# Holding back up to four score maxima to stand between dependent small VectorE instructions

## The chip, the cores and the metric

The kernel runs on one core of a Trainium2 chip. The metric is the device time of one execution in microseconds; the time of a kernel is the median of its runs. Lower is better.

## The reference

The program is attention that keeps the 32 largest scores of each row, followed by a mixture of experts with one expert per token. Shapes: q, k, v are 8 batches x 8 heads x 576 tokens x 64; eight experts of 512 x 1024 and 1024 x 512; all in float32.

```python
scores = scale * np.matmul(q, k.transpose(0, 1, 3, 2))
kth = np.partition(scores, -top_k, axis=-1)[..., -top_k:-top_k + 1]
mask = scores >= kth
scores = np.where(mask, scores, -1000000000.0)
...
attn = np.exp(scores)
attn = attn / (np.sum(attn, axis=-1, keepdims=True) + 1e-09)
return np.matmul(attn, v).astype(np.float32)
...
logits = x @ w_gate + modality_bias[modality_id]
e_idx = np.argmax(logits, axis=1)
...
    h = np.maximum(x[mask] @ w1[e], 0.0)
    out[mask] = gate_w[mask, None] * (h @ w2[e])
```

## The kernel before

The 64 heads are worked on as 32 pairs of heads of nine tiles each: 288 tiles of 128 query rows by 576 scores. One main loop takes one step per tile (line 846); the engines work on different tiles in the same step, by fixed offsets. In step i TensorE multiplies the scores of tile i+2 (`qk`, L324) and transposes the probabilities of tile i-9 (`trans`, L414); ScalarE makes the signs K of tile i-3 (`sign`, L369), the exponentials of tile i-6 (`expo`, L393) and copies the scores of tile i+2 to SBUF (`sevac`, L330); VectorE works on the score tile i. The attention output of a pair follows (`av`, L443), and whole experts of the mixture are fed to TensorE in the loop as soon as enough tokens are routed; a budget per step decides how many of their matrix products are issued (lines 931 to 942), by a table of costs and not by what runs late. After the loop (from about 1100 us) come the last batch's routing and the remaining expert slots.

The 32nd largest score of each row is found in parts. A row of 576 scores is cut in seven parts, and VectorE takes the eight largest of each (`subs`, L337, seven `MAX8` of 82 or 83 elements into `cand`, 56 candidates). In the next step the `chain` of that tile runs over the candidates: a `MAX8`, a replacement of the values found, a `MAX8`, a replacement, a `MAX8` (L348 to L350), each reading what the one before wrote. On the chip a replacement is two instructions, a load of the eight values (`MATCH_VALUE_LOAD`) and the replacement. GpSimd scales the 24th value (`below`, L362), ScalarE counts and signs with it, GpSimd multiplies scores and signs to `y` (L375), and VectorE takes the last eight maxima of `y` (`find`, L379). Every third step `pick` (L386 to L388) selects the threshold of three tiles with three small instructions, `eq`, `jk`, `kth`, each reading what the one before wrote. Last in every step `keep` (L399) compares the 576 scores with the threshold `kth` and multiplies with the exponentials; it writes the probabilities P.

The order on VectorE is written out by the loop (lines 949 to 982). `a_` holds the five instructions of the chain, `b_` the seven maxima, with `find` in its third place and the copies that came late (`lo`), and `c_` the step's end: `pick`, small instructions of the routing and of the choice of the next expert (`small_`, put at every second place, some of them DMAs or work of other engines), and `keep`. `weave` (L806) puts `a_` and `b_` into each other, one chain instruction first and then its share of `b_`; then `c_` runs as it stands:

```python
weave(a_, b_)
for f in c_:
    f()
```

The tile framework keeps this order on each engine and adds semaphore waits where an instruction reads what another one writes, on the same engine too. Score tiles lie in ten buffers (L329), the score PSUM tile in one, K in two, `y` in three. So ScalarE's copy of tile i+2 waits until VectorE's `keep` of tile i-8 has read the buffer's old tile.

Of the kernel before, what the change touches and what calls it, by code (L numbers as in the profile page):

```python
# [32 lines left out]
PJ = (0, 1, 3)  # L33
VJ = 7
QL = 2
KW = 8
KL = 2
LY = KL + 2
# [31 lines left out]
def kernel(  # L70
# [171 lines left out]
    def routing_loads():  # L242
        for h in range(2):
            SP.dma_start(wgt[h * 64:h * 64 + 64, :, h * E:h * E + E],
                         wg.rearrange("(a h p) e -> h p a e", h=2, p=64)[h])
        SP.dma_start(mbt, bass.AP(tensor=mb.tensor, offset=mb.offset, ap=[[0, 128], [E, 2], [1, E]]))
        pad_rows(E)
        return load_mod(0, B)
# [62 lines left out]
    def qk(i, p, j, bd):  # L311
        d = PR[p]
        ps = psS.tile([128, 2, 512], FT, name="S")
        for hf in range(2):
            a, b = hf * 288, hf * 288 + 288
            if j < 8:
                c, h = divmod(j, 2)
                terms = [(d["qs"][:, h, c * 128:(c + 1) * 128], x, h, a, b, 0) for x in range(2)]
            else:
                terms = [(bd[0], x, 0, a, b, 0) for x in range(2)]  # L320
                for u, v, o in ((a, min(b, 512), 64), (512, b, -512)):
                    terms += [(bd[1], x, 1, u, v, o) for x in range(2)] if u < v else []
            for n, (l, x, h, u, v, o) in enumerate(terms):
                PE.matmul(ps[:, hf, u - a:v - a], l, d["ks"][:, x, h, u + o:v + o], start=(n == 0),  # L324
                          stop=(n == len(terms) - 1), skip_group_check=(j == 8))
        T[i] = {"ps": ps}

    def sevac(i):
        T[i]["S"] = sb = wk.tile([128, S], FT, name="Ssb", bufs=LR + 1 + QL - QO)  # L329
        A.activation(sb.rearrange("p (a b) -> p a b", a=2), T[i]["ps"][:, :, :288], AF.Copy, scale=0.125)  # L330
# [64 lines left out]
    def keep(i, dn):  # L395

        t = T[i]
        probs(i)
        V.scalar_tensor_tensor(t["P"], t["S"], kth[:, i:i + 1], t["ex"], op0=OP.is_ge, op1=OP.mult, accum_out=dn)  # L399
# [5 lines left out]
    def probs(i):  # L405

        c, h = divmod(i % 9, 2)
        T[i]["P"] = Pm[:, :S] if c == 4 else Pb[c % 2][:, h * S:h * S + S]
# [15 lines left out]
    def av(p, j, x):  # L424

        vm, vt = LD[p]["v"]
        w = 256 if j < 8 else 64
        st = {}

        def part(c0, c1):  # L430
            if c0 == 0:
                st["po"] = psX.tile([128, 256], FT, name="X")
            po = st["po"]
            for c in range(c0, c1):
                for h in range(2):
                    K = slice(0, 128) if c < 4 else slice(64, 128) if h and j < 8 else slice(0, 64)
                    l = vm[:, h, c, :] if c < 4 else vt[K, h, :]
                    if j < 8:
                        r = PT[K, j // 2 - 1:j // 2 + 1, c + 5 * h if c < 4 else 4, :]
                    else:  # L440
                        r = PT[K, 1, 4 + c, h * 64:h * 64 + 64]
                    o = po[h * 64:h * 64 + 64, :w]
                    PE.matmul(o.rearrange("p (a b) -> p a b", a=2) if j < 8 else o, l, r, start=(c == 0), stop=(c == 4))  # L443
            if c1 == 5:
                o = (j // 4) * 256
                xev.append(lambda: A.activation(x[:, o:o + w], po[:, :w], AF.Copy))
        cut = {3: AV3, 7: AV7, 8: (0, 5)}[j]
        return [((b - a) * COST["av" if j < 8 else "av8"], lambda a=a, b=b: part(a, b)) for a, b in zip(cut, cut[1:])]
# [357 lines left out]
    def weave(a, b):  # L806

        nb, na, kb = len(b), len(a), 0
        for x in range(na):
            a[x]()  # L810
            e = (x + 1) * nb // na
            while kb < e:
                b[kb]()
                kb += 1
        while kb < nb:
            b[kb]()
            kb += 1

    def keep_warm(n):

        ps = psE.tile([128, 512], FT, name="E")
        for _ in range(2 * n):
            PE.matmul(ps[:, :256], onesb, idf.bitcast(BF), start=True, stop=True)
# [11 lines left out]
    modality = routing_loads()  # L835
    keep_warm(KW)
    for x in range(QL):
        qk(x, 0, x, qbd[0])
        sevac(x)
    ok = lambda x: 0 <= x < NT  # L840
# [5 lines left out]
    for i in range(LAST):  # L846
# [8 lines left out]
        def scores():  # L855
            if ok(i + QL):
                pp, jj = divmod(i + QL, 9)
                qk(i + QL, pp, jj, qbd[pp % 2])

        if ok(i + QL):  # L860
            cost += COST["mix" if (i + QL) % 9 == 8 else "qk"]
# [58 lines left out]
        if avs:  # L920
            c, f = avs.popleft()
            f()
            cost += c
        if ok(u) and u % 9 in (3, 7, 8):
            f = av(u // 9, u % 9, xTs(u // 36)[(u // 9) % HP])
# [6 lines left out]
        while seen[0] and spare_pe > 0:  # L932
# [4 lines left out]
            c, f, new = moe[0]  # L937
# [11 lines left out]
        a_, b_, c_ = [], [], []  # L949
# [11 lines left out]
        for x in range(RN if rush else 0):  # L961
            f = rush.popleft() if rush else PAUSE
# [6 lines left out]
        for x in range(SN - len(small_)):  # L969
            f = side.popleft() if side and not rush else PAUSE  # L970
# [6 lines left out]
        if ok(i - LR):  # L977
            u = i - LR
            c_.append(lambda u=u: keep(u, den[(u // 36) % 2][:, (u // 9) % HP, u % 9:u % 9 + 1]))
        weave(a_, b_)  # L980
        for f in c_:
            f()
# [269 lines left out]
```

## Time and profile before

| | |
|---|---|
| runs | 1340.63, 1344.9, 1348.74 us |
| median | 1344.9 us |
| the profiled execution | 1345.19 us, of which the span from first to last instruction is 1343.4 us |
| TensorE matmul busy | 1227.5 us (91%) |
| VectorE busy | 1174.4 us (87%) |
| ScalarE busy | 1001.1 us (75%) |
| GpSimd busy | 630.0 us (47%) |
| mean granted TensorE clock | 0.976 of full |

The profile is one execution, recorded by the hardware profiler. An instruction has a start and a duration; on VectorE the next one can start while the one before is still finishing, so the distance between two starts can be shorter than the duration, and the sum of durations is not the time that the engine needs. The views used below are the busy time by stretch, the lists of waits (who waited for whom, by semaphores) and the timeline, which gives each instruction's start and duration. In the rows PE is TensorE (PEld its weight loads), DVE VectorE, ACT ScalarE, POOL GpSimd and L a line of the kernel; [0.73 <-DVE P L399] behind an instruction says how long its engine had been idle and what ended that; in a list of waits the three numbers are the sum in us, how many, and the longest.

### The profile page before, as it was taken

The numbers are of one execution on the slowest core, as the hardware profiler recorded it, in microseconds if no ns is written. First come the engines' busy times: TensorE is split into PE (matmuls) and PEld (weight loads), VectorE is DVE, ScalarE is ACT, GpSimd is POOL, SyncE is SP. The second block draws the span as 40 slices with busy tenths as digits, with TensorE's granted clock in tenths as the row PEclk, the third lists the DMA queues.
The fourth block names the chain that finished last, engine by engine and source line by source line (L and its number), as shares of the span: only waits on it lengthen the run. The fifth ranks groups of instructions, "written<-read, shape, count | busy, mean of one in ns | idle before, by whom it ended". The sixth has DMA issues, their size and how long they took to land. (4 is left out here: it accounts for less than half of the span.)

```text
span 1343.4 us, 28995 instructions
## 1 busy us (share of the span) xinstructions
PE 1227.5 (91%) x8101; PEld 927.1 (69%) x8101; DVE 1174.4 (87%) x5958; ACT 1001.1 (75%) x1997; POOL 630.0 (47%) x1250
## 2 busy tenths in 40 slices
PE   6788887799998999999789999999999998999996
PEld 4666666576775867686567676876777665689985
DVE  3999999999999999999999999999999952666762
ACT  3788877888888879898888878988898851545642
POOL 2455547445565547554744575557554722011110
PEclk7899999899999999999989999999999999999998
DMA  5565334575545755653477556746664325656640
GB/s 118 137 177 124 81 81 115 147 198 142 135 116 163 201 134 160 185 142 81 131 189 193 134 157 165 176 112 196 166 176 126 124 80 177 219 181 228 236 170 15
DMA packets 206787, 201.05 MB, mean 150 GB/s; under 512 B 106221, under 2 KB 153325, under 8 KB 206608
## 3 DMA queue, kind: packets, MB, share of 16 engines
q1 hardware_dynamic: 200400, 179.48, 50.3%
q0 software_dynamic: 6208, 19.54, 4.0%
q8 instruction: 69, 1.13, 0.4%
q14 instruction: 110, 0.90, 0.2%
HBM read 118.63 MB, written 24.23 MB: 106 GB/s over the span
## 5 line engine op out<-in xcount | busy, mean ns | idle before, releaser
L337 DVE MAX8 cand<-Ssb 128x8 f32<-128x82 f32 (+1 forms) x2016 | 415.9, 229 | 19.9 <-ACT Ssb L330 19.8
L375 POOL TENSOR_TENSOR y<-Ssb,K 128x576 f32<-128x576 f32 x288 | 367.2, 1275 | 3.1 <-ACT K L369 2.6
L324 PE MATMUL S<-ks,qs 128*128 128x288 f32 x1024 | 234.9, 352 | 61.4 <-ACT Ssb L330 44.6
L330 ACT ACTIVATE Ssb<-S 128x576 f32<-128x576 f32 x288 | 187.9, 653 | 109.8 <-PE S L324 75.5
L369 ACT ACTIVATE K<-Ssb,n 128x576 bf16<-128x576 f32 x288 | 226.3, 786 | 31.2 <-POOL y L375 30.8
L324 PEld LDWEIGHTS S<-ks,qs 128*128 128x128 f32 x1024 | 160.0, 194 | 118.2 <-ACT Ssb L330 64.9
L393 ACT ACTIVATE ex<-Ssb,sm 128x576 f32<-128x576 f32 x288 | 224.2, 779 | 0.0
L399 DVE SCALAR_TENSOR_TENSOR P<-Ssb,kth,ex 128x576 f32<-128x576 f32 x256 | 213.5, 834 | 10.7 <-ACT ex L393 0.5
L379 DVE MAX8 mg<-y 128x8 f32<-128x576 f32 x288 | 213.8, 742 | 2.5 <-POOL y L375 2.5
L697 PE MATMUL E<-xgT,w1b 128*128 128x256 f32 x768 | 191.0, 392 | 6.7 <-ACT hT L701 4.5
L422 ACT ACTIVATE PT<-T 128x640 f32<-128x640 f32 (+1 forms) x288 | 190.0, 660 | 7.4 <-PE T L414 7.3
L709 PE MATMUL E<-w2b,hT 128*128 128x512 f32 x384 | 184.9, 605 | 2.2 <-ACT ot L719 1.3
L414 PE MATMUL T<-idf,P 128*128 128x128 f32 x1152 | 172.5, 277 | 0.0
L697 PEld LDWEIGHTS E<-xgT,w1b 128*128 128x128 f32 x768 | 140.6, 192 | 39.3 <-ACT hT L701 8.1
L443 PE MATMUL X<-PT,vm 128*64 128x256 f32 (+1 forms) x1536 | 163.2, 341 | 3.0 <-ACT st L260 2.5
L362 POOL TENSOR_SCALAR n<-mg 128x1 f32<-128x1 f32 x288 | 69.2, 240 | 201.9 <-DVE mg L350 198.2
L403 POOL TENSOR_SCALAR spare<-P 1x1 f32<-1x1 f32 x256 | 47.8, 187 | 219.4 <-DVE mg L348 204.2
L414 PEld LDWEIGHTS T<-idf,P 128*128 128x128 f32 x1152 | 138.0, 142 | 2.8 <-ACT PT L422 0.9
L443 PEld LDWEIGHTS X<-PT,vm 128*64 128x64 f32 x1536 | 80.8, 138 | 56.6 <-issue 27.0
L709 PEld LDWEIGHTS E<-w2b,hT 128*128 128x128 f32 x384 | 66.0, 190 | 64.2 <-issue 57.3
L1096 POOL DMA_INDIRECT out_dram<-ot,tk x14 | 14.0, 1003 | 131.0 <-ACT ot L1095 131.0
L348 DVE MAX8 mg<-cand 128x8 f32<-128x56 f32 x288 | 61.5, 214 | 0.2
(208 smaller groups left out, 2213.8 us busy)
## 6 DMA issues: line engine op xcount, KB each, us to landing
w1b<-in_moe_w_dram SPq DMA_DIRECT2D x76, 512.0 KB, 4.6
w2b<-in_moe_w_dram SPq DMA_DIRECT2D x76, 512.0 KB, 5.6
ks<-st SPq DMA_DIRECT2D x64, 288.0 KB, 3.9
qs<-st SPq DMA_DIRECT2D x128, 144.0 KB, 4.1
ks<-st SPq DMA_DIRECT2D x62, 256.0 KB, 5.0
xg<-xs SPq DMA_DIRECT2D x19, 516.0 KB, 5.9
km<-in_k_dram SPq DMA_DIRECT2D x64, 128.0 KB, 5.0
qm<-in_q_dram SPq DMA_DIRECT2D x64, 128.0 KB, 2.9
```

The lines of the kernel that those rows point to most:

```text
L324: PE.matmul(ps[:, hf, u - a:v - a], l, d["ks"][:, x, h, u + o:v + o], start=(n == 0), stop=(n == len(terms) - 1), skip_group_check=(j == 8))
L337: return [lambda s=s: V.max(c[:, s * 8:s * 8 + 8], T[i]["S"][:, bnd[s]:bnd[s + 1]]) for s in range(NSUB)]
L369: A.activation(t["K"], t["S"], AF.Sign, scale=2.0 ** -24 - 1.0, bias=t["n"][:, 1, i % 3:i % 3 + 1], accum_out=t["n"][:, 0, i % 3:i % 3 + 1])
L375: G.tensor_tensor(t["y"], t["S"], t["K"], op=OP.mult)
L379: V.max(t["mg"][:, i % 3, 24:32], t["y"])
L393: A.activation(t["ex"], t["S"], AF.Exp, bias=t["s"][:, i % 3:i % 3 + 1])
L399: V.scalar_tensor_tensor(t["P"], t["S"], kth[:, i:i + 1], t["ex"], op0=OP.is_ge, op1=OP.mult, accum_out=dn)
L414: PE.transpose(T[i]["pt"][:, x, :], (Pm if c == 4 else Pb[c % 2])[:, h * 512 + x * 128:h * 512 + x * 128 + 128], idf)
L422: A.activation(o, T[i]["pt"][:, :n], AF.Copy)
L443: PE.matmul(o.rearrange("p (a b) -> p a b", a=2) if j < 8 else o, l, r, start=(c == 0), stop=(c == 4))
L697: PE.matmul(ps[:, f % 2], w1b[:, c, f * 128:(f + 1) * 128], xgT[:, c, :], start=(c == 0), stop=(c == KC - 1))
L709: PE.matmul(o["py"], hT[:, f, t * 128:(t + 1) * 128], w2b[:, f, :], start=(f == 0), stop=(f == FC - 1))
```

## The change

```diff
+HOLD = 4
...
+        if ok(i) and len(c_) > 1:
+            n = min(len(c_) - 1, HOLD)
+            held, b_ = b_[len(b_) - n:], b_[:len(b_) - n]
+            m = len(c_) - n
+            c_ = c_[:m] + [f for pair in zip(held, c_[m:]) for f in pair]
         weave(a_, b_)
         for f in c_:
             f()
```

In a step whose end `c_` has more than one entry, the last n entries of `b_` (n is one less than the length of `c_`, at most four) are taken out of the weave and put one ahead of each of the last n entries of `c_`. No instruction is added or taken away. The order of TensorE, ScalarE, GpSimd and of the DMA queues is the same in both kernels; VectorE's alone changes. Lines from 36 on are one higher in the changed kernel, lines from 980 on seven higher.

First place: VectorE, the step that ends with the pick that the timeline below shows at 551.69 us; the first instruction of the weave, and the step's end. `cand` are the candidates, `mg` the chain's maxima. Before:

```order
L348 MAX mg<-cand 128x8
L337 MAX cand<-Ssb 128x8
L348 MATCH_REPLACE cand_9007<-mg,cand 128x56
...
L350 MAX mg<-cand_9008 128x8
L337 MAX cand<-Ssb 128x8 x2
L386 TENSOR_TENSOR eq<-i9s,n 128x27
L387 TENSOR_TENSOR jk<-eq,mg 128x27
L388 TENSOR_REDUCE kth<-jk 128x3
L399 SCALAR_TENSOR_TENSOR P_123,den_129<-Ssb,kth,ex 128x576
```

Changed:

```order
L349 MAX mg<-cand 128x8
L349 MATCH_REPLACE cand_9007<-mg,cand 128x56
L338 MAX cand<-Ssb 128x8
...
L387 TENSOR_TENSOR eq<-i9s,n 128x27
L338 MAX cand<-Ssb 128x8 x2
L388 TENSOR_TENSOR jk<-eq,mg 128x27
L338 MAX cand<-Ssb 128x8
L389 TENSOR_REDUCE kth<-jk 128x3
L338 MAX cand<-Ssb 128x8
L400 SCALAR_TENSOR_TENSOR P_123,den_129<-Ssb,kth,ex 128x576
```

Four maxima moved behind `eq`, `jk` and `kth`; with four taken out, the weave has none left for its first gap, and the chain's first maximum and the replacement that reads it stand side by side.

Second place: VectorE, the end of the step two before it, with two instructions of the expert choice (`s_sc` is the number of rows taken, `roff` the offset by expert). Before:

```order
L350 MAX mg<-cand_8890 128x8
L337 MAX cand<-Ssb 128x8 x2
L617 TENSOR_SCALAR s_sc<-s_sc 128x1
L618 SCALAR_TENSOR_TENSOR roff<-s_oh,s_sc,roff 128x8
L399 SCALAR_TENSOR_TENSOR P_122,den_129<-Ssb,kth,ex 128x576
```

Changed:

```order
L351 MAX mg<-cand_8890 128x8
L338 MAX cand<-Ssb 128x8 x2
L618 TENSOR_SCALAR s_sc<-s_sc 128x1
L338 MAX cand<-Ssb 128x8
L619 SCALAR_TENSOR_TENSOR roff<-s_oh,s_sc,roff 128x8
L338 MAX cand<-Ssb 128x8
L400 SCALAR_TENSOR_TENSOR P_122,den_129<-Ssb,kth,ex 128x576
```

One maximum now stands between the two instructions of the choice, and one ahead of `keep`.

In the whole loop, counted in the written order up to the 288th `keep`, pairs in which an instruction directly follows the one whose result it reads go from 73 to 4 for `eq`, `jk`; from 73 to 2 for `jk`, `kth`; from 82 to 2 for `kth`, `keep`; and by 87 for the other small instructions. Pairs of a chain maximum directly followed by the replacement that reads it go from 2 to 86.

## Rows read from the trace of the kernel before

**Rows 1.** Busy us by stretch: length, PE, PEld, DVE, ACT, POOL; TensorE clock, DMA share, GB/s.

```profile
40.00:300.00 260.00, 215.15 (x1646) 163.93 (x1644) 253.76 (x1367) 216.25 (x437) 135.84 (x267) 0.97 0.51 129
300.00:800.00 500.00, 476.18 (x3140) 349.64 (x3142) 486.44 (x2616) 421.14 (x865) 281.97 (x551) 0.98 0.58 150
800.00:1050.00 250.00, 245.95 (x1624) 179.67 (x1620) 245.06 (x1320) 211.37 (x438) 143.99 (x279) 1.00 0.60 158
1100.00:1343.00 243.00, 218.14 (x1289) 182.24 (x1289) 128.33 (x350) 100.38 (x158) 28.11 (x64) 0.96 0.50 169
```

**Rows 2.** VectorE's waits from 100 to 1050 us: sum in us, times, longest.

```profile
DVE x L477 <- PE X L476: 3.0, 2, 2.1
DVE mg L379 <- POOL y L375: 2.3, 3, 0.9
```

**Rows 3.** Timeline of VectorE at a plain pick: start, duration, then the instruction.

```profile
551.69 0.16 DVE L386 TENSOR_TENSOR eq<-i9s,n 128x27 f32<-128x27 f32 x1
551.89 0.19 DVE L387 TENSOR_TENSOR jk<-eq,mg 128x27 f32<-128x27 f32 x1
552.11 0.18 DVE L388 TENSOR_REDUCE kth<-jk 128x3 f32<-128x27 f32 x1
552.43 0.82 DVE L399 SCALAR_TENSOR_TENSOR P<-Ssb,kth,ex 128x576 f32<-128x576 f32 x1
...
553.17 0.21 DVE L348 MAX8 mg<-cand 128x8 f32<-128x56 f32 x1
553.30 0.23 DVE L337 MAX8 cand<-Ssb 128x8 f32<-128x82 f32 x1
553.45 0.07 DVE L348 MATCH_VALUE_LOAD cand<-mg,cand 128x8 f32 x1
```

**Rows 4.** Timeline of VectorE, a pick with routing instructions put between.

```profile
505.66 0.18 DVE L386 TENSOR_TENSOR eq<-i9s,n 128x27 f32<-128x27 f32 x1
505.78 0.20 DVE L558 TENSOR_REDUCE r_ps<-r_pr 128x5 f32<-128x40 f32 x1
505.90 0.20 DVE L387 TENSOR_TENSOR jk<-eq,mg 128x27 f32<-128x27 f32 x1
506.02 0.16 DVE L559 TENSOR_SCALAR dest<-r_ps 128x5 int32<-128x5 f32 x1
506.13 0.18 DVE L388 TENSOR_REDUCE kth<-jk 128x3 f32<-128x27 f32 x1
```

**Rows 5.** Timeline of VectorE, two routing instructions that read each other.

```profile
502.02 0.18 DVE L554 TENSOR_SCALAR r_sm<-r_sm 128x5 f32<-128x5 f32 x1
502.23 0.19 DVE L555 RECIPROCAL x<-r_sm 128x5 f32<-128x5 f32 x1
```

**Rows 6.** ScalarE's largest wait for VectorE, 40 to 300 us.

```profile
ACT Ssb L330 <- DVE P L399: 14.5, 18, 2.9
```

**Rows 7.** ScalarE's waits for VectorE and GpSimd, 300 to 800 us.

```profile
ACT K L369 <- POOL y L375: 15.0, 26, 2.8
ACT Ssb L330 <- DVE P L399: 6.7, 11, 1.2
...
ACT Ssb L330 <- DVE cand L337: 1.9, 2, 1.7
```

**Rows 8.** ScalarE's only wait for either, 800 to 1050 us.

```profile
ACT K L369 <- POOL y L375: 0.3, 1, 0.3
```

**Rows 9.** Timeline: a tile's score copy and its first maximum, tiles 43 and 261.

```profile
156.26 0.65 ACT L330 ACTIVATE Ssb<-S 128x576 f32<-128x576 f32 x1 [0.73 <-DVE P L399]
...
162.50 0.22 DVE L337 MAX8 cand<-Ssb 128x8 f32<-128x82 f32 x1
...
973.84 0.64 ACT L330 ACTIVATE Ssb<-S 128x576 f32<-128x576 f32 x1
...
975.47 0.23 DVE L337 MAX8 cand<-Ssb 128x8 f32<-128x82 f32 x1
```

**Rows 10.** Timeline of VectorE: the one long instruction of a pick.

```profile
517.46 1.18 DVE L387 TENSOR_TENSOR jk<-eq,mg 128x27 f32<-128x27 f32 x1
```

## The prediction

> **What bounds the kernel now.** I read the busy time by stretch first. From 40 to 1050 us VectorE is busy 253.76 of 260, 486.44 of 500 and 245.06 of 250 us; from 1100 us on, in the tail of expert slots, 128.33 of 243 [rows 1]. So the attention loop is the place, and the change acts nowhere else: maxima are held back only in steps that still have a tile of scores. Then the list of waits: from 100 to 1050 us VectorE waited 3.0 and 2.3 us for other engines, two more entries are under 1 us [rows 2]. In the loop it hardly waits for anybody. But TensorE is almost as full: 215.15 of 260 us in the first stretch, 476.18 of 500 in the second, 245.95 of 250 in the third, at a granted clock of 0.97, 0.98 and 1.00, which is the 2.4 GHz level [rows 1]. Two engines at the limit at once is the fact on which this prediction turns. The timeline last: it shows how busy time hides what the change is after. At a plain pick `eq` takes 0.16 us, and `jk`, which reads it, starts 0.20 us behind its start; `kth` follows after 0.22, `keep` after 0.32 [rows 3]. Where an instruction of something else stands between, starts are 0.12 us apart: `eq` to a routing sum, the sum to `jk`, `jk` to the next, and 0.11 once [rows 4]. So an independent follower overlaps the end of the one before, and a dependent one doesn't.
>
> **What a split pair is worth.** A maximum needs 0.15 us from its start to the next start (553.30 to 553.45) [rows 3], and it needs that wherever it stands. Standing in a dependent pair it lets the first instruction hand over after 0.12 [rows 4] and covers the rest. `eq` to `jk`: before 0.20 + 0.15 (the maximum elsewhere), after 0.12 + 0.15, saved 0.08. `jk` to `kth`: 0.22 against 0.12, saved 0.10. `kth` to `keep`: 0.12 + 0.15 is less than the 0.32 that `keep` waits, so the whole maximum disappears in it, saved 0.15. The other small pairs: 0.21 [rows 5] against 0.12, saved 0.09. By the written order 69, 71, 80 and 87 pairs of these kinds are split: 69 x 0.08 = 5.5, 71 x 0.10 = 7.1, 80 x 0.15 = 12.0, 87 x 0.09 = 7.8, together 32.4 us.
>
> **What it costs.** Steps that give up four maxima have none for the chain's first gap, and the load of the eight values to be replaced directly follows the maximum that finds them, in 84 more steps. Before, a maximum stood there: 553.17, 553.30, 553.45 [rows 3], so no row shows the pair alone. At the lower end the load starts 0.13 us behind, as the independent maximum does now, and costs nothing. At the upper end it is stretched as the one long `jk` was, which took 1.18 instead of 0.19 us [rows 10, 3]: 0.99 us. I take the price nearest to the other dependent pairs: the maximum's 0.21 us and the 0.04 by which `jk` starts behind the end of `eq`, 0.25 in place of 0.13 [rows 3]: 0.12 x 84 = 10.1 us. VectorE's own gain is then 32.4 - 10.1 = 22.3 us (32.4 at the lower end, a loss at the upper one).
>
> **What lies beside other work.** No engine has an instruction more. The maxima that move read a score tile that `keep` holds far longer, so no buffer comes free later. The chain's last maximum comes up to four maxima, 0.6 us, earlier in the step, which only helps GpSimd and the signs behind it. `find` moves later by about two short instructions, and whoever waits for its buffer (GpSimd) is busy 135.84 of 260 us [rows 1]. Costed at nothing.
>
> **How much of it reaches the end.** This depends on whether TensorE and ScalarE, which feed VectorE, could go faster. Where they can, they are seen waiting for VectorE. From 40 to 300 us the copy of the scores waited 14.5 us for `keep` to free a buffer [rows 6], and tile 43 lay ready from 156.26 + 0.65 = 156.91 to 162.50, 5.6 us before its first maximum [rows 9]. There the feeders run ahead as far as buffers let them, and VectorE's gain passes whole: 22.3 x 260/1010 = 5.7 us. From 300 to 800 us the copy waited 6.7 and 1.9 us for VectorE, and the signs 15.0 us for `y`, which GpSimd makes in VectorE's rhythm [rows 7]. VectorE would gain 22.3 x 500/1010 = 11.0 there. Between 0 and 11.0 I take 4.3, half of the direct 8.6, because such waits come in the lighter steps and the denser steps behind them use up the lead. From 800 to 1050 us the only wait of this kind is 0.3 us [rows 8]: the feeders run at their own pace. VectorE would gain 5.5, but can advance only by eating the lead, which at tile 261 was 975.47 - (973.84 + 0.64) = 0.99 us [rows 9]. I take 1.0. Beyond it VectorE will wait for scores or exponentials. Sum: 5.7 + 4.3 + 1.0 = 11.0 us. The tail starts when the loop's last work is done, on the same engines in the same order, so it moves by the same amount.
>
> The profiled execution took 1345.19 us, 0.3 over the median of the runs shown; 1345.2 - 11.0 = 1334.2, for a median of runs **1334**.
>
> **A rule against the change.** Instructions that read nothing of each other start 0.12 us apart although each takes 0.16 to 0.20 [rows 4], and a dependent one starts 0.04 us behind the end of its writer [rows 3]. The Trainium skill, VectorE: DVE Perf Modes, section "The DRAIN you can't avoid", says that after every VectorE instruction the next one doesn't start until the pipeline is empty, and that leaving out semaphores between chained instructions gained nothing in its measurement. By that rule a maximum between two dependent instructions would save nothing and the sum would be 0 in place of 22.3; by the rows it would be 22.3. I go by the rows, since the overlap is in them, and the rule keeps a small chance as the third rival.
>
> **The rivals.** First, the feeders bound everything from 300 us on: they keep their own pace and only the first stretch gains, 5.7 us, 1339.5. For it speaks TensorE's 245.95 of 250 us; against it the 8.6 us in which the feeders did wait for VectorE. Chance 0.20. Second, the feeders have more room than their busy time shows, as a matrix product that waits in the queue counts as busy: the whole 22.3 arrives, 1322.9. Against it speaks the lead that shrinks from 5.6 to 1.0 us [rows 9], which an engine with room would keep. Chance 0.15. Third, the spacing gives nothing, since a dependent instruction's delay moves with it to the next start: 1345. Against it, [rows 4]. Chance 0.05. Fourth, on the other side: the uncovered load in the chain is dear. Per step it decides at 32.4 / 84 = 0.39 us; at 0.50 it is 42.0 - 32.4 = 9.6 us lost, 1355, and at 0.99 far more, since VectorE has no cover for it in a loop where it is the bound. For it speaks that no row shows this pair; against it that all dependent pairs seen cost 0.08 to 0.20. Chance 0.05. My forecast has 0.55.
>
> **How the numbers follow.** About 0.5%, 6.7 us, is what a measurement of this kernel can tell from no change. Forecast and second rival are faster by more than that: 0.70. The first rival (5.7) and the third are within it: 0.25. The fourth is slower: 0.05. The range goes from the second rival, 1322 with the rounding of its terms, to just beyond the first, 1341; it leaves out the third and the fourth and the outer edges of both others.
>
> **What would show it.** `jk` and `kth` should start within 0.30 us of the instruction before them with a maximum between; `keep` about 0.32 us behind `kth`; the load of the values 0.25 us behind its maximum. In the third stretch VectorE should show new waits for scores or exponentials, several us in all where there were none, and TensorE should fill 98 to 99% of it. The last `keep` should come about 11 us earlier. If VectorE shows no new waits and the time falls by 20 us or more, the feeders had room and the second rival holds. If the load starts 0.39 us or more behind its maximum, the fourth does. If the maxima between pairs leave the distance between `eq` and `kth` grown by their full 0.15 each, the third does.

## The result, and the profile after

The changed kernel takes 1330.66 us (median of seven runs, 1325.47 to 1333.5), the kernel before 1345.14 (seven runs, 1340.63 to 1348.74). The ratio is 0.9883 with a 95% interval from 0.9855 to 0.9911: 14.5 us by the medians, 12.0 to 19.5 by the interval. The forecast was 1334, a gain of 11.0. The changed kernel's profiled execution took 1326.14 us, 4.5 below its median, so its trace shows a larger gain (19.1 us) than the medians do; sums that are read from traces below are too large by about that much for the median.

Busy time by stretch of the changed kernel, columns as in [rows 1]:

```profile
40.00:300.00 260.00, 223.49 (x1693) 170.74 (x1695) 258.56 (x1421) 223.06 (x452) 141.18 (x278) 0.96 0.54 136
300.00:800.00 500.00, 480.29 (x3192) 352.80 (x3188) 489.74 (x2652) 424.78 (x877) 286.66 (x561) 0.99 0.59 154
800.00:1050.00 250.00, 247.01 (x1622) 179.94 (x1619) 242.57 (x1316) 213.22 (x441) 146.23 (x284) 1.00 0.58 155
```

In the third stretch TensorE went from 245.95 to 247.01 of 250 us, VectorE from 245.06 to 242.57: TensorE now has the less room of the two.

VectorE's waits from 100 to 1050 us, of the changed kernel:

```profile
DVE x L478 <- PE X L477: 6.5, 6, 1.7
DVE lt L506 <- PE X L498: 4.0, 5, 1.6
DVE mg L380 <- POOL y L376: 2.8, 6, 0.6
DVE P L400 <- ACT ex L394: 0.8, 2, 0.5
...
DVE cand L338 <- ACT Ssb L331: 0.2, 1, 0.2
```

Before there were 3.0 and 2.3 us of them, and two under 1 us [rows 2]; all entries together went from 6.4 to 15.1 us. The new ones are for TensorE, at the copies of transposed token rows (L478) and of the logits' rows (L506); for scores and exponentials it is 0.2 and 0.8 us.

The timeline of VectorE in the changed kernel, at the pick of [rows 3]; first the uncovered load (the one that directly follows its maximum), then the pick, then the loop's last probabilities:

```profile
536.38 0.21 DVE L349 MAX8 mg<-cand 128x8 f32<-128x56 f32 x1
536.63 0.09 DVE L349 MATCH_VALUE_LOAD cand<-mg,cand 128x8 f32 x1
...
538.35 0.17 DVE L387 TENSOR_TENSOR eq<-i9s,n 128x27 f32<-128x27 f32 x1
538.44 0.38 DVE L338 MAX8 cand<-Ssb 128x8 f32<-128x83 f32 x2
538.74 0.17 DVE L388 TENSOR_TENSOR jk<-eq,mg 128x27 f32<-128x27 f32 x1
538.82 0.24 DVE L338 MAX8 cand<-Ssb 128x8 f32<-128x82 f32 x1
538.98 0.17 DVE L389 TENSOR_REDUCE kth<-jk 128x3 f32<-128x27 f32 x1
539.06 0.24 DVE L338 MAX8 cand<-Ssb 128x8 f32<-128x83 f32 x1
539.28 0.82 DVE L400 SCALAR_TENSOR_TENSOR P<-Ssb,kth,ex 128x576 f32<-128x576 f32 x1
...
1075.76 0.82 DVE L400 SCALAR_TENSOR_TENSOR Pm<-Ssb,kth,ex 128x576 f32<-128x576 f32 x1 [2.68 <-ACT ex L394]
```

`eq` hands over after 0.09 us, `jk` and `kth` after 0.08; `keep` still starts 0.30 behind `kth`, with the maximum inside that time. The load starts 0.25 us behind its maximum, with nothing in between. The same last instruction of the kernel before:

```profile
1094.58 0.82 DVE L399 SCALAR_TENSOR_TENSOR Pm<-Ssb,kth,ex 128x576 f32<-128x576 f32 x1 [2.55 <-ACT ex L393]
```

The loop's last probabilities come 18.8 us earlier. What follows takes 248.6 us of the span in place of 248.8, at a granted clock of 0.96 in both: the tail only moved. In some of the traces below the same instructions of the tail ran at a granted clock of 0.98 and took less, 243.9 us in the bunched kernel and 245.5 with HOLD 3. So the place of the last probabilities tells more of the loop than the time of one execution does. Counted at every 72nd `keep`, the gain is 1.6 us at the first, then 11.1 (301.66 to 290.60 us), 13.8, 19.4 and 18.8: more than half of it is made in the first quarter of the steps.

ScalarE's largest waits for VectorE and GpSimd in the changed kernel, first from 300 to 800 us, then from 800 to 1050:

```profile
ACT K L370 <- POOL y L376: 5.6, 14, 0.9
...
ACT Ssb L331 <- DVE P L400: 3.5, 7, 0.9
```

```profile
ACT K L370 <- POOL y L376: 1.0, 1, 1.0
```

From 300 to 800 us the 15.0 and 6.7 us of [rows 7] fell to 5.6 and 3.5: the time in which the feeders could have run faster was largely used up.

### The profile page after: what moved, and what is told of

It reads as the page before. It is cut to its first block, busy times and chain, and to the rows that moved or that the text cites. A ratio compares the mean times of both kernels' runs of the same rounds, so it can differ in the third digit from the quotient of the medians.

```text
span 1324.3 us, 28995 instructions
## 1 busy us (share of the span) xinstructions
PE 1223.4 (92%) x8101; PEld 925.3 (70%) x8101; DVE 1162.7 (88%) x5958; ACT 998.3 (75%) x1997; POOL 628.0 (47%) x1250
## 5 line engine op out<-in xcount | busy, mean ns | idle before, releaser
L338 DVE MAX8 cand<-Ssb 128x8 f32<-128x82 f32 (+1 forms) x2016 | 432.0, 231 | 19.2 <-ACT Ssb L331 19.2
```

Of the source, the lines that this page charges most:

```text
L338: return [lambda s=s: V.max(c[:, s * 8:s * 8 + 8], T[i]["S"][:, bnd[s]:bnd[s + 1]]) for s in range(NSUB)]
```

## The experiments

The theory: spacing dependent pairs saves VectorE time, uncovered loads cost some of it, and TensorE's work in the dense stretches takes back about a third of the rest. HOLD is the largest number of maxima held back in a step. All experiments are edits of the changed kernel, but for the light kernel before, which is one of the kernel before; the times of the kernel before stand beside each from the same chip.

**Bunched: the maxima held back, but not between the pairs.**

```diff
-            c_ = c_[:m] + [f for pair in zip(held, c_[m:]) for f in pair]
+            c_ = held + c_
```

> The same maxima are taken out of the weave, but all put ahead of the step's end instead of between its instructions, so no dependent pair is split, the chain still ends early and the 84 uncovered loads stay. Theory (spacing is what pays): VectorE loses 84 x 0.115 = 9.7 us and nothing is gained, 6 to 10 us slower than the kernel before, and the load starts 0.25 us behind its maximum. Rival (it pays that the chain ends up to 0.6 us earlier for GpSimd and ScalarE): faster than before by most of the 14.5 us of the change.

Measured 1351.15 us against 1344.81, ratio 1.005 [1.0034, 1.0067]. The loop's last probabilities:

```profile
1103.15 0.82 DVE L400 SCALAR_TENSOR_TENSOR Pm<-Ssb,kth,ex 128x576 f32<-128x576 f32 x1 [2.40 <-ACT ex L394]
```

They come 8.6 us later than before; 84 loads at 0.115 make 9.7. The medians are 6.3 us apart. So the earlier end of the chain brings little or nothing, the uncovered loads cost about what was reckoned, and the gain of the change is in the splitting.

**HOLD 3: the weave keeps a maximum for each gap of the chain.**

```diff
-HOLD = 4
+HOLD = 3
```

> HOLD is 3 instead of 4, so the weave keeps a maximum for each gap of the chain: no uncovered load, and the split pairs are 68, 71, 80 and 68 instead of 69, 71, 80 and 87. Theory (VectorE still bounds a good part of the loop): its own gain rises from 30 to 37 us by the measured distances, and half to all of the 7 arrives: 18 to 22 us faster than before, 3 to 7 faster than the change. Rival (TensorE and ScalarE bind after the change): the same as the change within 2 us, with new waits of VectorE.

Measured 1327.4 us against 1344.81, ratio 0.9878 [0.9848, 0.9907], not to be told from the change's 0.9883. The last probabilities come when they came with 4, and VectorE waits more, though no load is uncovered:

```profile
1075.76 0.82 DVE L400 SCALAR_TENSOR_TENSOR Pm<-Ssb,kth,ex 128x576 f32<-128x576 f32 x1 [2.80 <-ACT ex L394]
```

```profile
DVE x L478 <- PE X L477: 9.5, 8, 3.1
DVE lt L506 <- PE X L498: 3.6, 4, 1.7
DVE mg L380 <- POOL y L376: 3.6, 6, 0.7
```

The 18 to 22 us were not quite reached in the median (17.4). The median is 3.3 us under the change's, which the theory allowed and the rival didn't, but the loop ends at the same time in both traces: there the 3.0 us between the spans lie in the tail, at its other granted clock. In the loop it is the rival's result.

**Light kernels: TensorE relieved, before and after the change.** In both, half of the contraction of the first expert product is left out in the loop.

```diff
-            for c in range(c0, c0 + HG):
+            for c in range(c0, c0 + HG, 2):
...
-                          start=(c == 0), stop=(c == KC - 1))
+                          start=(c == 0), stop=(c == KC - 2))
```

TensorE's matmul busy time in the whole kernel falls by it from 1227.5 to 1166.7 us (kernel before and light kernel before).

> The kernel before with half of the first expert product left out in the loop (two of four contraction slices, lines 696 to 698; the expert slots behind the loop are whole), so TensorE has some 80 us less to do beside the attention. Theory (VectorE bounds the loop before the change): the last probabilities come within 10 us of where they came (1094.6 us), and the time falls by 5 to 20 us, some 8 of them in the last slot behind the loop. Rival (TensorE sets the pace already before): the loop alone falls by over 20 us.

> The changed kernel with the same half of the first expert product left out. Theory (TensorE and ScalarE took back some 10 of VectorE's 30 us): with TensorE relieved 24 to 30 us lie between this and the light kernel before. Rival (they take back nothing and VectorE's own gain is only what arrived): the difference is the 14 to 19 us of the whole kernels.

Measured 1334.83 us without the change and 1307.26 with it: 27.6 us apart, ratios to the kernel before (1344.81) 0.9919 [0.9892, 0.9946] and 0.9727 [0.97, 0.9753]. The last probabilities of the light kernel before, then of the light changed kernel:

```profile
1093.20 0.81 DVE L399 SCALAR_TENSOR_TENSOR Pm<-Ssb,kth,ex 128x576 f32<-128x576 f32 x1
```

```profile
1065.04 0.82 DVE L400 SCALAR_TENSOR_TENSOR Pm<-Ssb,kth,ex 128x576 f32<-128x576 f32 x1
```

Without the change the relief moves them by 1.4 us (from 1094.58): VectorE was the loop's bound. The tail, with less to do as well, is some 9 us shorter in both light kernels (239.7 and 239.4 us), so it doesn't count between them. With TensorE relieved the change is worth 28.2 us in the loop in place of 18.8. This is the clearest result of the study: VectorE's own gain is about 28 us, and in the whole kernel TensorE kept 9.4 of it by the traces, 13.1 by the medians (27.6 against 14.5). What it kept shows as VectorE's waits: 8.7 us more of them with the change in the whole kernel; in the light changed kernel the two at copies of TensorE's rows are down again (100 to 1050 us):

```profile
DVE x L478 <- PE X L477: 3.6, 3, 3.1
...
DVE lt L506 <- PE X L498: 0.4, 1, 0.4
```

The traces also show where TensorE kept it. The gain of the change in us, at the start of every 72nd `keep`:

| `keep` | whole kernels | light kernels |
|---|---|---|
| 1st | 1.6 | 1.3 |
| 73rd | 11.1 | 10.3 |
| 145th | 13.8 | 15.7 |
| 217th | 19.4 | 21.8 |
| last | 18.8 | 28.2 |

Up to the 217th, TensorE kept 2.4 us; about 7 of the 9.4 it kept in the last quarter of the steps.

**HOLD 3 in the light kernel.** The two edits above together.

> HOLD 3, with the same half of the first expert product left out in the loop as in the two light kernels. Theory (HOLD 3 does save VectorE 7 us more, and in the whole kernel TensorE and ScalarE took all of it: the last probabilities came at 1075.8 us with 3 and with 4): relieved, the last probabilities come 5 to 8 us earlier than in the light changed kernel (1065.0 us), and the time is some 6 us less than its 1307.3. Rival (an uncovered load costs nothing that counts, HOLD 3 saves nothing): 1307 within 2 us.

Measured 1305.92 us against 1344.96, ratio 0.9701 [0.967, 0.9733], within the noise of the light changed kernel; the last probabilities come 1.0 us earlier:

```profile
1064.03 0.81 DVE L400 SCALAR_TENSOR_TENSOR Pm<-Ssb,kth,ex 128x576 f32<-128x576 f32 x1
```

The 5 to 8 us expected didn't come. Added up from the starts in the timelines, the chain's first maximum and the load behind it take 10.4 us less than in the light changed kernel, as they should. Against it, 2.1 us go to the 19 small pairs that three maxima no longer split, VectorE's waits grow by 5.0 us (8.1 to 13.1, most of it for TensorE and GpSimd), and 1.6 us go to more instructions stretched beside GpSimd (25 in place of 22, see the last section). That leaves 1.7, near the 1.0 measured. So the saving was there and was used up elsewhere; why the waits grow even with TensorE relieved stays open, and half of one product left out may relieve it too little.

**Pick steps alone, and the other steps alone.**

```diff
-        if ok(i) and len(c_) > 1:
+        if ok(i) and ok(i - LT) and (i - LT) % 3 == 2:
```

```diff
-        if ok(i) and len(c_) > 1:
+        if ok(i) and len(c_) > 1 and not (ok(i - LT) and (i - LT) % 3 == 2):
```

> HOLD 4, but maxima are held back only in the steps that end with a pick (96 of 288). Theory (own gain by the measured distances 69 x 0.11 + 71 x 0.13 + 80 x 0.17 less 51 uncovered loads x 0.115, 24.5 of 30 us; the feeders take back a third or more): 11 to 15 us faster than before. Rival (the routing's small instructions matter most, as they stand in the steps that are dense for TensorE too): under 8 us faster.

> HOLD 4, but only in the steps without a pick. Theory: 84 x 0.11 less 33 uncovered loads x 0.115 is 5.4 us of own gain, and of it 0 to 5 arrive: within 0.5% of before. Rival as in the run before: over 8 us faster.

Measured 1331.12 us for the pick steps, ratio 0.9896 [0.9864, 0.9927], and 1339.96 for the others, 0.9982 [0.9962, 1.0002], beside 1344.96. Both are as the theory had them; the second can't be told from no change. In the traces the last probabilities come 11.7 us earlier than before with the pick steps (1082.89 us) and 3.4 with the others (1091.16), of the 18.8 with both. Most of the gain comes from the 96 steps with a pick, as the sum of its pairs had it.

**More expert work per step.** HOLD 3 with:

```diff
-STEP = 3.3
+STEP = 3.5
```

> HOLD 3 and the budget of expert work per step 3.5 instead of 3.3, so that more of the experts' products stand in the loop's first dense stretches and 24 fewer behind the last scores. Theory (TensorE's work is the bound in the dense stretches, but it idles some 6 to 10 us at 400 to 500 and 600 to 700 us): where expert work is there to fill these, 2 to 6 us less than HOLD 3 alone (1327). Rival (the dense stretches only grow denser and VectorE waits more): 0 to 6 us slower than HOLD 3.

Measured 1331.94 us against 1344.96, ratio 0.9896 [0.9866, 0.9926], 4.5 us over HOLD 3 by the medians: the rival's side. VectorE's waits of this kernel from 40 to 1050 us:

```profile
DVE x L478 <- PE X L477: 18.1, 16, 2.6
DVE lt L506 <- PE X L498: 5.4, 6, 1.5
DVE P L400 <- ACT ex L394: 3.8, 6, 1.5
```

The wait at the copies of transposed rows goes from 9.5 to 18.1 us when TensorE gets more to do in the loop, as it went down when TensorE got less: it is a wait for TensorE's capacity.

**Late copies later, and the pick dealt out.** HOLD 3 with the copies three maxima later in the weave; HOLD 3 with another order in the pick steps, where the chain's last maximum and four held maxima stand between the small instructions (`s_` are the routing's, which in this kernel no longer stand at every second place, `pk` is eq, jk, kth, `a_[4]` the chain's last maximum); and both. Of the second edit only two lines are shown.

```diff
-LOP = (2, 5, 8, 10, 12)
+LOP = (5, 6, 8, 10, 12)
```

```diff
...
+            t_ = [s_[0], pk[0], a_[4], s_[1], held[0], pk[1], s_[2], held[1], pk[2], s_[3], held[2], held[3]]
+            a_ = a_[:4]
...
```

> HOLD 3, and the copies that came late (the rows that TensorE transposed in the step before) stand at place 5 instead of 2 of the weave, three maxima later. HOLD 3 alone waited 9.5 us at them and 3.6 at the logits' rows. Theory (they wait because they stand early in a step in which TensorE is late): the wait at them falls below 3 us, the last probabilities come 4 to 8 us earlier than 1075.8 us, and the time is 4 to 8 us under HOLD 3. Rival (TensorE is simply behind in these stretches, wherever VectorE meets it): the wait turns up elsewhere or the lead shrinks, the time is that of HOLD 3 within 2 us.

> HOLD 3 in the steps without a pick; in a step with one, four maxima and the chain's last maximum are dealt out between the three small instructions, two of them ahead of the last one, and every gap of the chain keeps a maximum. Theory (VectorE's own gain grows by some 7 us over HOLD 3, as the rest of the wait behind kth and the waits of jk go): with the feeders taking most of it, 0 to 4 us under HOLD 3. Rival (own gain still arrives in full): 6 to 8 us under HOLD 3.

> Both edits of the two runs before together. If each removes a wait of its own, 4 to 10 us under HOLD 3, about 1318 to 1323; if TensorE's work in the dense stretches is the floor, 1325 to 1329 as HOLD 3.

Measured 1324.93, 1325.19 and 1324.65 us beside a kernel before of 1348.3, ratios 0.9829 [0.9802, 0.9856], 0.9831 [0.9812, 0.985] and 0.9823 [0.9796, 0.9851]. With the copies later, VectorE waits (40 to 1050 us):

```profile
DVE x L478 <- PE X L477: 5.2, 6, 1.8
DVE lt L506 <- PE X L498: 3.9, 5, 1.1
DVE mg L380 <- POOL y L376: 3.6, 6, 0.7
DVE P L400 <- ACT ex L394: 2.0, 4, 0.7
DVE cand L338 <- ACT Ssb L331: 1.7, 2, 1.4
```

4.3 us leave the copies (9.5 to 5.2, not below 3 as the theory had it), 1.5 and 0.8 turn up at the probabilities and the first maxima, and the last probabilities come at 1077.33 us, 1.6 later than with HOLD 3: in the trace the rival's prediction. With the pick dealt out they come at 1073.78, 2.0 earlier; with both at 1077.12. So in the loop the two edits do not add up, as edits against one floor don't. All three are faster than the kernel before. Their medians lie 5 to 6 us under the changed kernel's, though the kernel before was 3.2 us slower beside them, so by the ratios they gain 7 to 8 us on the change; the traces don't show where, since the loop ends within 2 us of the change's in all three. The dealt-out pick is the best candidate, with the earliest end of the loop and an interval that ends at 0.985 where the change's begins at 0.9855; that it beats the change is likely, not settled, and for the late copies theory and rival stay undecided between time and trace.

## Why the prediction was right, and where its sizes were off

**What bounds the kernel** was right on both sides. VectorE bounded the loop before: relieving TensorE alone moved the loop's end by 1.4 us. TensorE stood close behind: relieved, it let 28.2 us through in place of 18.8.

**What a split pair is worth** was sized too low. The hand-over was taken as 0.12 us from [rows 4], whose instructions were read as independent of each other. They are two chains put into each other: `r_ps` reads `r_pr`, which stands just ahead of `eq`, and `dest` reads `r_ps`.

```profile
505.56 0.18 DVE L557 TENSOR_TENSOR r_pr<-r_pb,ohb 128x40 f32<-128x40 f32 x1
```

So each of the rows starts 0.22 to 0.24 us behind the one that it reads, two places ahead, near the dependent distance (the median is 0.22 where `r_ps` directly follows `r_pr`), and 0.12 is about half of that. What an independent follower needs stands in the changed kernel: medians of its starts are 0.086 behind `eq` and `jk` and 0.079 behind `kth`. The following `jk` starts 0.156 behind its maximum and `keep` up to 0.22, so the pairs save 0.11, 0.13 and 0.17 in place of 0.08, 0.10 and 0.15, the others about 0.11. With the counts of the written order: 69 x 0.109 + 71 x 0.126 + 80 x 0.17 + 87 x 0.11 = 39.6 us. The **cost** was nearly right: 0.25 us from maximum to load, 84 x 0.115 = 9.7 against 10.1 reckoned. An uncovered load also hands over later, after 0.078 in place of 0.060 us, which makes 1.5 more; the bunched kernel showed the cost by itself. Own gain 28.4 us by this sum, 28.2 by the light kernels, 22.3 predicted: the mis-sized term.

**How much reaches the end.** For the first stretch 5.7 us were predicted, the whole own gain there; the gain at the 73rd `keep` is 11.1, of which 1.6 stood at the first already. Part of that error is the own gain itself; the rest is that it was spread evenly. In the written order, 11 of the 84 uncovered loads and 22 or 23 of each pick pair lie in the first 72 steps, so with the measured distances about 9.5 of the 28 us belong there, and the light kernels gained 9.0. For 300 to 800 us 4.3 were taken, two fifths of the own gain there; to the 217th `keep`, near 820 us, 8.3 came, of 11.6 in the light kernels, and the fraction was too small. For the last stretch 1.0 was taken; -0.6 came, of about 6 in the light kernels. The mechanism, full passage first and almost none last, was right. No two errors cancelled: own gain and passage in the middle were both sized too low, so the forecast lies on the low side of the 14.5 us, and further below the 18.8 of the trace.

**The new wait** came, but not where it was looked for: VectorE waits at copies of rows that TensorE transposed (6.5 and 4.0 us), not for scores or exponentials (0.2 and 0.8). The rows stand behind other work in TensorE's own queue and are read in VectorE's next step, while scores come two steps ahead. **The tail** moved unchanged, as said, between these two traces.

**The rivals.** The first (gain in the first stretch only) and the second (all arrives) are both out: about half of the own gain arrived by the medians (14.5 of 27.6), two thirds by the traces (18.8 of 28.2). The third is refuted by its own sign: from `eq` to `kth` it is 0.63 us with three maxima between, which need 0.45, in place of 0.42 without. The rule of the Trainium skill (VectorE: DVE Perf Modes, "The DRAIN you can't avoid") that the next instruction waits for an empty pipeline doesn't describe these independent followers, which start after 0.08 us; the same section adds that an instruction which isn't held starts earlier, and that fits them. The fourth's price was measured at 0.13 us, far under the 0.39 from which it decides. (The sign for it named 0.39 us from maximum to load; with the 0.13 that stood there already it should have been 0.52. The measured 0.25 is under both.)

## What to carry to other kernels

On an engine that looks 97% busy, compare the distances of starts, not the durations: a dependent small instruction here started 0.20 to 0.32 us behind its writer, an independent one after 0.08 to 0.12, and independent work that must be done anyway fills the difference. Make sure that an "independent" follower in the rows really is one, and doesn't wait for an instruction two places ahead. Take the filler from where it covers nothing, since each gap it leaves open elsewhere costs about what a filled one brings (0.13 us here, against 0.11 to 0.17). Before hoping for all of the gain, look at how far ahead the feeding engines run: here the gain passed where their lead was full, and the next engine kept it where the lead was about 1 us.

## What the runs showed of the hardware that was not expected

The long `jk` of [rows 10], from 517.46 to 518.64 us, was taken as an upper price for a dependent pair. It was something else. GpSimd's multiplication in the kernel before, at the same time:

```profile
517.32 1.28 POOL L375 TENSOR_TENSOR y<-Ssb,K 128x576 f32<-128x576 f32 x1
```

It ends at 518.60, 0.04 us before `jk` does. In the kernel before 24 instructions of `eq`, `jk` and `keep` are stretched so (`eq` and `jk` over 0.4 us, `keep` over 1.0), and in the changed kernel 23. Each overlaps a multiplication of GpSimd: a stretched `eq` or `jk` ends 0.04 to 0.05 us after it, a stretched `keep` 0.62 us after it. What they take beyond their usual 0.17, 0.19 and 0.82 us is about 15 us per execution in both kernels. The one-input maxima that run beside the same multiplication aren't stretched. In the changed kernel there is also one `keep` with which it is the other way round:

```profile
1032.29 0.82 DVE L400 SCALAR_TENSOR_TENSOR P<-Ssb,kth,ex 128x576 f32<-128x576 f32 x1
1032.45 1.80 POOL L376 TENSOR_TENSOR y<-Ssb,K 128x576 f32<-128x576 f32 x1
```

`keep` started first and took its usual time, and the multiplication took 1.80 in place of 1.27 us. The Trainium skill, SBUF — State Buffer, section "Who interferes with whom", says that a VectorE instruction with two SBUF inputs contends with a GpSimd instruction that reads SBUF, and that one with at most one SBUF input, outside VectorE's two-port modes, does not. The traces agree: of `eq`, `jk`, `keep` and the maxima only the first three, with two inputs, were stretched, and each past the multiplication's end. No run here moved the multiplication away, so the cause stays inferred from the times.
